# The output product of a fused attention and feed-forward kernel by Strassen's seven products

## The chip, the cores and the metric

One Trainium2 chip, one core of it. The metric is device time in microseconds (us) of one execution, the median of several runs. Engines are named as the profile names them: PE (matmuls), PEld (its weight loads), DVE (vector), ACT (scalar), POOL (GpSimd), and SP, whose queue issues the loads and stores.

## The reference

A decayed linear attention (retention) over 4 batches, 8 heads, 768 tokens, 64 channels a head, and then a bilinear feed-forward over all 3072 tokens:

```python
for t in range(S):
    state = gamma[None, :, None, None] * state + np.einsum('bhd,bhe->bhde', k[:, :, t], v[:, :, t])
    y[:, :, t] = scale * np.einsum('bhd,bhde->bhe', q[:, :, t], state)
...
a = x @ w_a          # x: 3072 x 512, w_a and w_b: 512 x 1536
b = x @ w_b
return (a * b @ w_out).astype(np.float32)     # w_out: 1536 x 512
```

Inputs and output are float32; the kernel multiplies in bfloat16 and accumulates in float32.

## The kernel before, in words

The 3072 tokens are 24 slots of 128. `TILES = [4, 2, 2, 2, 2, 4, 4, 4]` groups them into eight tiles, numbered J = 0 to 7, of 512 or 256 tokens. Everything is written out once in Python; `seq` ties each instruction to the one before it on its engine, so that every engine runs its instructions in the order of the program, and what sets that order is where a call stands.

A tile has two parts. **Its blocks**: for each of the 12 slices `ft` of the 1536 hidden channels, `ffn_a` makes four matmuls into a PSUM bank and ACT copies the result to `asb` (L540); `ffn_g` makes four more and DVE multiplies them with `asb` into `ht` (L551). **Its out part**: `ffn_out` (L566) makes, for each slot, 12 matmuls of 512 columns (`ht` against `wo_bf`), and ACT copies the bank to `osb` (L180), which SP stores. The tags of PSUM allow three banks for all of `a`, `g`, `o` and half of the state products (pool `psff`, `bufs=3`): a new product can start only when the reader of the bank that it takes is done.

The attention of two slots is a `turn` (L354), put between such calls by the table `ahead`. On PE it takes the old pair's products with the states (`inter`, twice) and within the chunk (`intra`), and the new pair's state products (`chunk_states`) and scores. On DVE it leaves a tiny copy that orders two groups of matmuls (`fenced`, L297), three or four running sums of states (`sums`, L269) and two masks (`aT`, L285). The casts of the sums to `gst` (mostly ACT) and the two copies of the attention's output to `xt` (`leave`, L343) go to a list, `later`, that `catch_up` empties at the next `ffn_out`, or two at a time at each `ft`. `xt[J]` is what the blocks of tile J read. Slots 10 and 11, for instance, are attended in a turn in the out part of tile 3 and are tile 4.

Loads of the weights go through staging tiles of the pool `wstage` (`wst`), which POOL casts to bfloat16; those of `w_out` by `cast_o`, before the blocks of tile 1. The order is: attention of the first slots and the blocks of tile 0; the blocks of tile 1; the out parts of tiles 0 and 1; and then for each tile 2 to 7 its blocks and its out part.

Of the kernel before, what the change touches and what calls it, by code (L numbers as in the profile page):

```python
# [16 lines left out]
PAIRS = 3  # L17
# [6 lines left out]
def kernel(  # L24
# [57 lines left out]
    def load_slot(t, names="kqv"):  # L82
        b, ci = divmod(t, NCH)
        for nm in names:
            if t % 2 == 0:
                whole[nm] = raw.tile([P, 2, H, D], F32, tag=nm + "f", name=nm + "f")
            raws[nm, t] = whole[nm][:, t % 2]
            s = {"k": k, "q": q, "v": v}[nm][b, :, ci * P : (ci + 1) * P, :]
            seq(nc.sync.dma_start(out=raws[nm, t], in_=s.rearrange("h p d -> p h d")))
# [46 lines left out]
    def tables(pattern, channel):  # L136
        posp = const.tile([P, NCH, 1], F32, name=f"posp{channel}")
        seq(nc.gpsimd.iota(posp, pattern=pattern, base=-MID, channel_multiplier=channel,
                           allow_small_or_imprecise_dtypes=True))
        earg = const.tile([P, NCH, H], F32, name=f"earg{channel}")  # L140
        seq(nc.vector.tensor_tensor(earg, posp.to_broadcast([P, NCH, H]),
                                    lgr.to_broadcast([P, NCH, H]), op=ALU.mult))
        ktab = const.tile([P, NCH, H, 1], F32, name=f"ktab{channel}")
        qtab = const.tile([P, NCH, H, 1], F32, name=f"qtab{channel}")
        seq(nc.scalar.activation(ktab[:, :, :, 0], earg, AF.Exp, scale=-1.0))
        seq(nc.scalar.activation(qtab[:, :, :, 0], earg, AF.Exp, bias=bq))
        tabs.append((ktab, qtab))

    tables([[2 * P, PAIRS], [1, 2], [0, 1]], 2)
# [15 lines left out]
    def late_tables():  # L165
        seq(nc.gpsimd.memset(mask, 1.0))
        for c in range(2):
            mc = mask[64 * c : 64 * c + 64]
            seq(nc.gpsimd.affine_select(out=mc, in_=mc, compare_op=ALU.is_ge, fill=0.0, base=0,
                                        pattern=[[0, 1], [1, D]], channel_multiplier=-1))  # L170
        tables([[P, NCH], [0, 1]], 1)
# [4 lines left out]
    wo_bf = wpool.tile([P, NFT, DM], BF16, name="wo_bf")  # L176
# [13 lines left out]
    def cast_o(j):  # L190
        cast(nc.gpsimd, wo_bf[:, j * FPO : (j + 1) * FPO, :], wst["o", j])
# [41 lines left out]
    def half(i):  # L233
        return slice(64 * i, 64 * i + 64)

# [37 lines left out]
    def scores(n):  # L273
        at = psat.tile([P, 2, 2, HP, D], F32, tag="at", name="at")
        for s in range(2):
            for hp in range(HP):
                for c in range(2):
                    for r in range(2):
                        seq(nc.tensor.matmul(at[half(c), r, s, hp, :],  # L279
                                             kqT[n + s][half(r), 0, hp, half(c)],  # L280
                                             kqT[n + s][half(r), 1, hp, half(c)],
# [28 lines left out]
    def inter(o, swap, y):  # L310

        for s in range(2):
            for j in range(2):
                for r in range(2):
# [4 lines left out]
                    for hp in (2 * j, 2 * j + 1):  # L319
                        into(o, c, r, seq(nc.tensor.matmul(  # L320
                            y[c][half(hp % 2), s, 2 * r + j, :], gst[(2 * t + c) % 8][half(r), hp, :],
                            kqT[t][half(r), 1, hp, half(c)], stop=y is not ys[o],
# [13 lines left out]

    def leave(o, c, apart):
        J, i = where[o]
        if i == 0 and c == 0:
            xt[J] = xtp.tile([P, KT, 4 * P], BF16, tag="xt", name="xt")  # L340
        dst = xt[J][:, :, i * P : (i + 2) * P].rearrange("p k (s c n) -> p c s k n", s=2, c=2)[:, c]
        if apart is None:
            seq(nc.scalar.copy(dst, ys[o][c]))  # L343
        else:
            on, off = slice(2 - 2 * c, 4 - 2 * c), slice(2 * c, 2 * c + 2)
            part = tra.tile([P, 2, 2, D], F32, tag="kq"[c] + "T2", name="part", bufs=2)
            seq(nc.scalar.copy(part, apart[c][:, :, on]))
            for s in range(2):
                seq(nc.vector.tensor_tensor(dst[:, s, on], ys[o][c][:, s, on], part[:, s], op=ALU.add))
                seq(nc.scalar.copy(dst[:, s, off], ys[o][c][:, s, off]))  # L350
# [128 lines left out]
    def leave2(u, on):  # L479
        J, i = where[2 * u]  # L480
        if i == 0 and J not in xt:
            xt[J] = xtp.tile([P, 4, KT, P], BF16, tag="xt", name="xt")
        for c, eng in enumerate(on):
            if eng is None:
                continue
            cast(eng, xt[J][:, i + c].rearrange("p k (m par) -> p k par m", par=2),
                 ys[u][c].rearrange("p k (par m) -> p k par m", par=2))

    def leave_apart(u, apart):

        J, i = where[2 * u]
        dst = xt[J][:, i + 1].rearrange("p k (m par) -> p k par m", par=2)
# [5 lines left out]
        seq(nc.vector.tensor_copy(dst[:, 2:], y[:, 2:]))  # L498

    def xcols(J, kt, c0, c1):  # L500
        if J < 2:
            return xt[J][:, c0 // P : c1 // P, kt, :]
        return xt[J][:, kt, c0:c1]
# [61 lines left out]

    def ffn_out(J, i):  # L566
        store()
        catch_up()
        n0 = (sum(TILES[:J]) + i) * P
        osb = wstage.tile([P, DM], F32, tag="w" + "ab"[i % 2], name="osb")  # L570
        ends = J == len(TILES) - 1 and i == TILES[J] - 1
        cols = [(0, DM // 2), (DM // 2, 3 * DM // 4), (3 * DM // 4, DM)] if ends else [(0, DM)]
        for c0, c1 in cols:
            o = psff.tile([P, DM], F32, tag="ff", name="o")[:, : c1 - c0]
            for ft in range(NFT):
                seq(nc.tensor.matmul(o, ht[J][:, ft, i * P : (i + 1) * P], wo_bf[:, ft, c0:c1],  # L576
                                     start=(ft == 0), stop=(ft == NFT - 1)))
            cast(nc.vector if c0 == DM // 2 else nc.scalar, osb[:, c0:c1], o)
            if c0 == DM // 2:
                continue  # L580
            b0 = DM // 2 if c0 else 0
            dst, src = out[n0 : n0 + P, b0:c1], osb[:, b0:c1]
            if J < len(TILES) - 2:
                held.append((dst, src))
            else:
                seq((nc.scalar if ends and not c0 else nc.sync).dma_start(out=dst, in_=src))
# [116 lines left out]
    def run(*at):  # L703
        for fn, *what in ahead.pop(at, []):
            fn(*what)
        if len(at) == 2:
            ffn_ab(*at)
        else:
            ffn_out(at[0], at[2])

    for ft in range(NFT):
        run(1, ft)
    for J in range(len(TILES)):
        if J > 1:
            for ft in range(NFT):
# [38 lines left out]
```

## Time and profile before

| | |
|---|---|
| Time of three runs | 223.96, 224.16, 224.42 us; median 224.16 |
| Span of the profiled execution | 222.2 us, granted clock 1.000 |
| Profiled execution's own time | not listed apart; the median lies 1.96 us above the span |
| PE busy | 214.4 us (96%) |
| DVE, ACT, POOL busy | 96.8, 93.7, 79.5 us |
| Chain that ended last | PE 92%; `g` 28%, `a` 28%, `o` 28% |

Busy time is the time in which an engine ran at least one instruction. A row of a group gives the count, the busy time in us and the mean duration of one in ns; for a matmul that duration holds the passage through the array, so neighbours overlap, and the rate is read from the distance of starts. After "|" stands the idle time of the engine ahead of the group and what ended it.

### The profile page before, as it was taken

To read this page: it belongs to the slowest core of one execution; us is meant where nothing else is said; L and a number is where in the kernel's file an instruction comes from. 1 tells how busy PE (TensorE), PEld (TensorE's weight loads), DVE (VectorE), ACT (ScalarE), POOL (GpSimd) and SP (SyncE) were. 2 spreads that over 40 slices of the span, in tenths; PEclk is the share of its full clock that TensorE was granted. 3 is DMA by queue.
4 is the path that set the end of the run, shared out by engine and by line. 5 is a ranking of instruction groups with operands and counts; after the bars stand their busy time and mean duration, and the time that the engine had idled before them with its cause. 6 is when DMAs were issued, how large, how long until landed. Compare 5 with 4: busy or idle time off the path is not lost.

```text
span 222.2 us, 6261 instructions
## 1 busy us (share of the span) xinstructions
PE 214.4 (96%) x2613; PEld 131.3 (59%) x2633; DVE 96.8 (44%) x199; ACT 93.7 (42%) x201; POOL 79.5 (36%) x105
## 2 busy tenths in 40 slices
PE   7799999999999999999999999999999999999994
PEld 6578655785457867867865444554444544444443
DVE  2783437641525535472475344533333621334300
ACT  3775244441535435443456333455333444333221
POOL 5557799682544335351613535350000000000000
PEclk9999999999999999999999999999999999999999
DMA  6999999999999988999969898984100012100022
GB/s 180 347 378 382 366 312 398 299 210 200 228 236 266 242 197 129 227 211 204 219 145 228 115 248 220 216 181 131 47 0 0 3 50 94 47 3 0 3 94 94
DMA packets 96124, 39.72 MB, mean 179 GB/s; under 512 B 76000, under 2 KB 91616, under 8 KB 96096
## 3 DMA queue, kind: packets, MB, share of 16 engines
q1 hardware_dynamic: 95952, 39.20, 68.5%
q8 instruction: 20, 0.33, 0.6%
q10 hardware_dynamic: 144, 0.13, 0.2%
q14 instruction: 8, 0.07, 0.1%
HBM read 28.31 MB, written 6.29 MB: 156 GB/s over the span
## 4 chain that ended last, share of the span: by engine, by line
PE 92%; DMA 3%; POOL 1%; issue 1%; DVE 1%; SPq 0%; ACT 0%; ACTq 0%; POOLq 0%
PE g L548 28%; PE a L536 28%; PE o L576 28%; DMA kf<-in_k_dram 3%; PE y L320 1%; POOL kqb L210 1%; PE at L279 1%; PE y L332 1%; PE st L255 1%; PE tp L395 1%; PE st L436 1%; DVE aT L420 1%; SPq L95 0%; PE at L408 0%; PE y L459 0%
## 5 line engine op out<-in xcount | busy, mean ns | idle before, releaser
L551 DVE TENSOR_TENSOR ht<-g,asb 128x256 bf16<-128x256 f32 (+1 forms) x98 | 53.9, 550 | 82.6 <-PE g L548 73.4
L548 PE MATMUL g<-xt,wb_bf 128*128 128x256 bf16 (+1 forms) x401 | 77.5, 317 | 0.2
L536 PE MATMUL a<-xt,wa_bf 128*128 128x256 bf16 (+1 forms) x401 | 77.2, 317 | 0.1
L540 ACT CAST asb<-a 128x256 bf16<-128x256 f32 (+1 forms) x98 | 46.3, 472 | 71.3 <-PE a L536 69.3
L576 PE MATMUL o<-wo_bf,ht 128*128 128x512 bf16 (+2 forms) x299 | 62.5, 362 | 1.4 <-issue 1.1
L536 PEld LDWEIGHTS <-wa_bf 128*128 128x128 bf16 x404 | 39.2, 98 | 23.5 <-DVE xt L182 0.4
L548 PEld LDWEIGHTS <-wb_bf 128*128 128x128 bf16 x404 | 39.4, 98 | 22.5
L576 PEld LDWEIGHTS <-ht 128*128 128x128 bf16 x312 | 28.8, 98 | 30.6
L210 POOL TENSOR_TENSOR kqb<-kf,ktab 128x512 bf16<-128x512 f32 x21 | 22.3, 1065 | 39.9 <-DMA kf<-in_k_dram 31.5
L180 ACT COPY osb<-o 128x512 f32<-128x512 f32 (+2 forms) x25 | 14.1, 564 | 36.1 <-PE o L576 27.8
L182 POOL CAST vb<-vf 128x512 bf16<-128x512 f32 x24 | 14.4, 610 | 23.0 <-DMA vf<-in_v_dram 18.5
L210 POOL TENSOR_TENSOR kqb<-qf,qtab 128x512 bf16<-128x512 f32 x21 | 22.3, 1063 | 0.1
L269 DVE TENSOR_TENSOR sums<-st,sums 128x256 f32<-128x256 f32 x30 | 12.7, 424 | 1.6
L180 ACT CAST gst<-sums 128x256 bf16<-128x256 f32 x26 | 10.4, 406 | 5.1 <-DVE sums L269 2.4
L285 DVE TENSOR_TENSOR aT<-at,mask 128x512 bf16<-128x512 f32 x18 | 11.5, 681 | 0.0
L343 ACT CAST xt<-y 128x512 bf16<-128x512 f32 x16 | 8.5, 584 | 0.7 <-PE y L332 0.7
L182 POOL CAST wo_bf<-wsto 128x1024 bf16<-128x1024 f32 x6 | 6.2, 1040 | 2.5 <-DMA wsto<-in_moe_w_out_dram 2.5
L182 POOL CAST wa_bf<-wsta 128x1024 bf16<-128x1024 f32 (+1 forms) x7 | 6.4, 919 | 1.7 <-DMA wsta<-in_moe_w_a_dram 1.6
L182 POOL CAST wb_bf<-wstb 128x1024 bf16<-128x1024 f32 (+1 forms) x7 | 6.4, 918 | 1.5 <-DMA wstb<-in_moe_w_b_dram 1.3
L395 PE MATMUL tp<-ident,kqb 128*128 128x128 bf16 x48 | 4.5, 220 | 1.6 <-DVE kqb L210 0.9
L320 PEld LDWEIGHTS <-gst 64*64 64x64 bf16 x264 | 3.7, 106 | 3.4 <-issue 3.4
L297 DVE COPY lgr<-bq 128x1 f32<-128x1 f32 x4 | 0.6, 154 | 11.2 <-PE y L320 11.2
(63 smaller groups left out, 99.2 us busy)
## 6 DMA issues: line engine op xcount, KB each, us to landing
out_dram<-osb SPq DMA_DIRECT2D x23, 256.0 KB, 2.7
kf<-in_k_dram SPq DMA_DIRECT2D x18, 256.0 KB, 4.2
qf<-in_q_dram SPq DMA_DIRECT2D x18, 256.0 KB, 4.4
vf<-in_v_dram SPq DMA_DIRECT2D x18, 256.0 KB, 4.9
wsta<-in_moe_w_a_dram SPq DMA_DIRECT2D x6, 512.0 KB, 7.6
wstb<-in_moe_w_b_dram SPq DMA_DIRECT2D x6, 512.0 KB, 7.8
wsto<-in_moe_w_out_dram SPq DMA_DIRECT2D x6, 512.0 KB, 8.5
kf<-in_k_dram SPq DMA_DIRECT2D x3, 512.0 KB, 5.9
```

The source lines that it names most:

```text
L180: seq(nc.scalar.copy(dst, src))
L182: seq(engine.tensor_copy(dst, src))
L210: seq(eng.tensor_tensor(dst, src, tab, op=ALU.mult))
L269: seq(nc.vector.tensor_tensor(new, u[c][:, s], old, op=ALU.add))
L285: seq(nc.vector.tensor_tensor(aT[n][:, r].rearrange("p s h d -> p (s h) d"), at[:, r].rearrange("p s h d -> p (s h) d"), mask.to_broadcast ...
L343: seq(nc.scalar.copy(dst, ys[o][c]))
L395: seq(nc.tensor.transpose(tp[:, m, hp, :], kqb[2 * u + par][:, i, hp, :, :], ident))
L536: seq(nc.tensor.matmul(a[:, b0 - c0 : b1 - c0], wa_bf[:, kt, fs], xcols(J, kt, b0, b1), start=(kt == 0 and b0 == c0), stop=(kt == KT - 1 a ...
L540: seq(nc.scalar.copy(asb, a))
L548: seq(nc.tensor.matmul(g[:, b0 - c0 : b1 - c0], wb_bf[:, kt, fs], xcols(J, kt, b0, b1), start=(kt == 0 and b0 == c0), stop=(kt == KT - 1 a ...
L551: seq(nc.vector.tensor_tensor(ht[J][:, ft, c0:c1], g, asbs.pop((J, ft, c0)), op=ALU.mult))
L576: seq(nc.tensor.matmul(o, ht[J][:, ft, i * P : (i + 1) * P], wo_bf[:, ft, c0:c1], start=(ft == 0), stop=(ft == NFT - 1)))
```

## The change

Tiles 1 to 7 no longer take 12 matmuls of 512 columns a slot. Two slots (256 tokens, a pair `u`) are split into even and odd tokens, the hidden channels into two halves of six slices, the output columns into two halves of 256; Strassen's method makes the 2 x 2 block product with seven half-size products instead of eight. Each product is six matmuls of 256 columns. They are called P1 to P7 here, in the order in which `ffn_fast` has them:

- P1 (bank R1) and P2 (bank R6) take `ht` as it is. ACT copies P1 to `snap` (snapshot 0), and DVE adds P2 and it into `osb`.
- P3 goes on top of P1 in R1, with the second sum of `ht` halves; ACT takes snapshot 1. P4 (bank R5), with the first sum; snapshot 2.
- P5 on top in R1, with the third sum; DVE adds it and snapshot 2. P6 on top in R5, with the fourth; DVE adds it and snapshot 1. P7 on top in R1, with `ht` as it is; ACT copies it to `osb`.

So a product that goes on top waits for the reader of what was there: P3 for snapshot 0, P5 for snapshot 1, P6 for snapshot 2, P7 for DVE's add of P5.

The four sums of `ht` halves (`hsum`, bfloat16) are DVE's: the first two in pieces among the last blocks of the tile (`sums12`), the others per pair ahead of it (`sums34`). The four combinations of the halves of `w_out` (`wt_bf`) are made once, by `combine_o`: four DVE instructions and an ACT cast for each of six slices, two slices among the blocks of tile 1, four behind the first two out products of tile 0 (which keeps the old `ffn_out`). `later` is emptied one entry at a time between products (`catch_up(1)`), and wholly at the end of a pair. A turn that stood ahead of an odd slot of a pair now stands inside it, between P3 and P4 (tiles 1, 2 and 4). So that even and odd tokens lie apart, `q` of the late slots is loaded by two DMAs instead of one (even and odd tokens), `queries` reads the turned `q` in two runs of 32, and the copies to `xt` are written in that order; a store is one of 512 KB a pair instead of two of 256 KB.

```diff
@@ load_slot
+            if nm == "q":
+                s = s.rearrange("h (n par) d -> par n h d", par=2)
+                for par in range(2):
+                    seq(nc.sync.dma_start(out=raws[nm, t][64 * par : 64 * par + 64], in_=s[par]))
...
+    def combine_o(j):
+        st = wst["o", j].rearrange("p r (c d) -> p r c d", c=2)
+        b11, b12, b21, b22 = st[:, 0, 0], st[:, 0, 1], st[:, 1, 0], st[:, 1, 1]
+        tmp = tra.tile([P, 2, DH], F32, tag="aT", name="tmp")
+        seq(nc.vector.tensor_tensor(tmp[:, 0], b12, b11, op=ALU.subtract))
+        seq(nc.vector.tensor_tensor(tmp[:, 1], b22, tmp[:, 0], op=ALU.subtract))
+        seq(nc.vector.tensor_tensor(wt_bf[:, j, 2], b22, b12, op=ALU.subtract))
+        seq(nc.vector.tensor_tensor(wt_bf[:, j, 3], b21, tmp[:, 1], op=ALU.subtract))
+        seq(nc.scalar.copy(wt_bf[:, j, :2], tmp))
...
+    def sums12(J, f0, f1):
+        if f0 == 0:
+            hsum[J] = [new_hsum(i) for i in range(2)]
+        s = [x[:, f0:f1, : TILES[J] // 2] for x in hsum[J]]
+        seq(nc.vector.tensor_tensor(s[0], rows(J, 0, 1, f0, f1), rows(J, 1, 1, f0, f1), op=ALU.add))
+        seq(nc.vector.tensor_tensor(s[1], s[0], rows(J, 0, 0, f0, f1), op=ALU.subtract))
+
+    def sums34(J, u):
...
+        seq(nc.vector.tensor_tensor(s[2], at[0], at[1], op=ALU.subtract))
+        seq(nc.vector.tensor_tensor(s[3], at[2], s[1], op=ALU.subtract))
...
+    def ffn_fast(J, u, between=None):
+        store()
+        catch_up(1)
...
+        R1 = bank()
+        product(R1, J, u, ("h", 0, 0), (0, 0), True)
+        seq(nc.scalar.copy(snap[:, 0], R1[:, :DH]))
+        catch_up(1)
+        R6 = bank()
+        product(R6, J, u, ("h", 1, 0), (0, 2), True)
+        seq(nc.vector.tensor_tensor(osb[:, 0, :DH], R6[:, :DH], snap[:, 0], op=ALU.add))
+        catch_up(1)
+        product(R1, J, u, ("s", 1), (1, 1), False)
+        seq(nc.scalar.copy(snap[:, 1], R1[:, :DH]))
+        if between:
+            between()
+        else:
+            catch_up(1)
+        R5 = bank()
+        product(R5, J, u, ("s", 0), (1, 0), True)
+        seq(nc.scalar.copy(snap[:, 2], R5[:, :DH]))
+        catch_up(1)
+        product(R1, J, u, ("s", 2), (1, 2), False)
+        seq(nc.vector.tensor_tensor(osb[:, 1, DH:], R1[:, :DH], snap[:, 2], op=ALU.add))
...
+        catch_up(1)
+        product(R5, J, u, ("s", 3), (0, 3), False)
+        seq(nc.vector.tensor_tensor(osb[:, 0, DH:], R5[:, :DH], snap[:, 1], op=ALU.add))
...
+        catch_up(1)
+        product(R1, J, u, ("h", 1, 1), (1, 3), False)
+        seq(nc.scalar.copy(osb[:, 1, :DH], R1[:, :DH]))
+        catch_up()
...
+            if J == 1 and ft in (5, 9):
+                combine_o(ft // 4 - 1)
+            if J and TILES[J] == 2 and ft in (8, 10, 11):
+                sums12(J, *{8: (0, 3), 10: (3, 5), 11: (5, 6)}[ft])
+            if J and TILES[J] == 4 and ft in (7, 9, 10, 11):
+                sums12(J, *{7: (0, 2), 9: (2, 4), 10: (4, 5), 11: (5, 6)}[ft])
...
+        for u in range(TILES[J] // 2):
+            sums34(J, u)
+            visit(J, "o", 2 * u)
+            key = (J, "o", 2 * u + 1)
+            ffn_fast(J, u, (lambda: visit(*key)) if key in ahead else None)
```

How the order moves is shown at three places; a row is one instruction, or several alike, in its engine's order, with output, input and shape.

ACT at the blocks of tile 1 and the start of the out part of tile 0, before:

```order
L180 CAST xt<-y 128x4x2x64
L540 CAST asb<-a 128x256 x12
L180 COPY osb<-o 128x512 x2
L180 CAST gst_161<-sums 128x256
L180 CAST gst_162<-sums 128x256
```

And with the change (`tmp` and `wt_bf` are those of `combine_o`):

```order
L195 CAST xt<-y 128x8x64
L575 CAST asb<-a 128x256 x6
L217 CAST wt_bf<-tmp 128x512
L575 CAST asb<-a 128x256 x4
L217 CAST wt_bf<-tmp 128x512
L575 CAST asb<-a 128x256 x2
L621 COPY osb<-o 128x512
L217 CAST wt_bf<-tmp 128x512 x2
```

The copies `asb` of `ft` 6 and 10 now stand behind a cast that reads what DVE makes.

ACT from the blocks of tile 2 to the first out product of tile 3, before (`xt` is the pair of copies that the next tile's blocks read, `lgr` the ordering copy of a turn):

```order
L540 CAST asb<-a 128x256 x12
L180 COPY osb<-o 128x512
L180 CAST gst_161<-sums 128x256
L180 CAST gst_162<-sums 128x256
L343 CAST xt<-y 128x2x4x64 x2
L180 COPY osb<-o 128x512
L540 CAST asb<-a 128x256 x12
L297 COPY lgr<-bq 128x1
L180 CAST gst_157<-sums 128x256
L180 CAST gst_158<-sums 128x256
L343 CAST xt<-y 128x2x4x64 x2
L180 COPY osb<-o 128x512 x2
```

And with the change:

```order
L575 CAST asb<-a 128x256 x12
L672 COPY snap<-o 128x256
L679 COPY snap<-o 128x256
L686 COPY snap<-o 128x256
L195 CAST gst_161<-sums 128x256
L195 CAST gst_162<-sums 128x256
L699 COPY osb<-o 128x256
L376 CAST xt<-y 128x2x8x32 x2
L575 CAST asb<-a 128x256 x12
L326 COPY lgr<-bq 128x1
L195 CAST gst_157<-sums 128x256
L672 COPY snap<-o 128x256
```

In tile 2 the two copies to `xt` moved from ahead of the last output copy to behind it; in tile 3 a `gst` cast stands ahead of snapshot 0.

DVE from the end of the blocks of tile 4 through its out part, which holds two turns, before:

```order
L551 TENSOR_TENSOR ht<-g,asb 128x256 x12
L269 TENSOR_TENSOR sums<-st,sums 128x256 x4
L285 TENSOR_TENSOR aT<-at,mask 128x512 x2
L182 CAST gst_163<-sums 128x256
L182 CAST gst_156<-sums 128x256
L297 COPY lgr<-bq 128x1
L269 TENSOR_TENSOR sums<-st,sums 128x256 x3
L285 TENSOR_TENSOR aT<-at,mask 128x512 x2
```

And with the change, from the last `ht` on (`hsum` are the sums of `ht` halves, `osb<-o,snap` the adds of `ffn_fast`):

```order
L586 TENSOR_TENSOR ht<-g,asb 128x256
L638 TENSOR_TENSOR hsum<-ht 128x128
L639 TENSOR_TENSOR hsum<-hsum,ht 128x128
L646 TENSOR_TENSOR hsum<-ht 128x6x128
L647 TENSOR_TENSOR hsum<-ht,hsum 128x6x128
L298 TENSOR_TENSOR sums<-st,sums 128x256 x4
L314 TENSOR_TENSOR aT<-at,mask 128x512 x2
L676 TENSOR_TENSOR osb<-o,snap 128x256
L197 CAST gst_163<-sums 128x256
L197 CAST gst_156<-sums 128x256
L326 COPY lgr<-bq 128x1
L298 TENSOR_TENSOR sums<-st,sums 128x256 x3
```

Four sums of `ht` stand between the last `ht` and the turn's state sums, and the add of P2 ahead of the two `gst` casts.

187 lines of the change are left out of this document (120 added, 67 removed).

## The prediction

> **What bounds the kernel now.** The page first: shares of busy time, the slices, the chain.
>
> ```profile
> PE 214.4 (96%) x2613; PEld 131.3 (59%) x2633; DVE 96.8 (44%) x199; ACT 93.7 (42%) x201; POOL 79.5 (36%) x105
> PE   7799999999999999999999999999999999999994
> PEclk9999999999999999999999999999999999999999
> PE 92%; DMA 3%; POOL 1%; issue 1%; DVE 1%; SPq 0%; ACT 0%; ACTq 0%; POOLq 0%
> ```
>
> PE is full from the third slice to the last at full clock, and is 92% of the chain: every matmul less shortens the kernel by its length, and every wait of PE lengthens it. DVE and ACT stand under half, but that is a mean over the span; what counts is the few us of each out part.
>
> The groups with shapes kept apart then give the prices.
>
> ```profile
> L576 PE MATMUL o<-wo_bf,ht 128*128 128x512 bf16 x263 | 59.9, 379 | 1.4 <-issue 1.1
> L551 DVE TENSOR_TENSOR ht<-g,asb 128x512 bf16<-128x512 f32 x46 | 31.8, 692 | 55.1 <-PE g L548 55.1
> L551 DVE TENSOR_TENSOR ht<-g,asb 128x256 bf16<-128x256 f32 x52 | 22.1, 425 | 27.5 <-PE g L548 18.3 <-ACT asb L540 9.2
> L540 ACT CAST asb<-a 128x256 bf16<-128x256 f32 x52 | 19.4, 372 | 23.5 <-PE a L536 22.6 <-DVE ht L551 0.6
> L180 ACT COPY osb<-o 128x512 f32<-128x512 f32 x23 | 13.5, 586 | 34.4 <-PE o L576 26.1 <-DMA out_dram<-osb 4.0 <-DMA kf<-in_k_dram 2.0
> L269 DVE TENSOR_TENSOR sums<-st,sums 128x256 f32<-128x256 f32 x30 | 12.7, 424 | 1.6
> L180 ACT CAST gst<-sums 128x256 bf16<-128x256 f32 x26 | 10.4, 406 | 5.1 <-DVE sums L269 2.4 <-DVE sums L267 1.5
> L180 ACT CAST vb<-vf 128x512 bf16<-128x512 f32 x1 | 0.6, 622 | 0.0
> L180 ACT COPY osb<-o 128x256 f32<-128x256 f32 x1 | 0.4, 373 | 0.7 <-PE o L576 0.7
> ```
>
> Before, an out product waits for nothing: 1.4 us idle over all of them.
>
> **What is saved.** The rate of 512-column matmuls is read from the distance of two output copies, that of 256-column ones from the chain; the last rows of this fence are stretches of a 256-column tile.
>
> ```profile
> 211.32 0.58 ACT L180 COPY osb<-o 128x512 f32<-128x512 f32 x1 [2.87 <-PE o L576]
> 213.91 0.59 ACT L180 COPY osb<-o 128x512 f32<-128x512 f32 x1 [2.00 <-DMA out_dram<-osb]
> 68.92 0.44 PE g L548 x4
> 73.29 0.44 PE g L548 x4
> 41.00 0.60 PE L536 MATMUL a<-xt,wa_bf 128*128 128x256 bf16 x4
> 41.43 0.60 PE L548 MATMUL g<-xt,wb_bf 128*128 128x256 bf16 x4
> 41.63 0.37 ACT L540 CAST asb<-a 128x256 bf16<-128x256 f32 x1 [0.54 <-PE a L536]
> 41.87 0.60 PE L536 MATMUL a<-xt,wa_bf 128*128 128x256 bf16 x4
> 42.14 0.42 DVE L551 TENSOR_TENSOR ht<-g,asb 128x256 bf16<-128x256 f32 x1 [0.49 <-PE g L548]
> 39.27 0.74 DVE L182 CAST xt<-y 128x512 bf16<-128x512 f32 x1
> 40.07 0.61 PE L536 MATMUL a<-xt,wa_bf 128*128 128x256 bf16 x4
> ```
>
> A slot's 12 matmuls take 2.59 us, a pair's 24 take 5.18. From 68.92 to 73.29 lie five rounds of a and g, 40 matmuls: 0.109 us each, weight loads included. Seven products of six are 42 x 0.109 = 4.59, one product 0.655. Saved: 0.59 a pair, **5.9 us** over ten pairs.
>
> **What a reader costs.** ACT starts 0.20 after the matmuls' last issue (41.43 to 41.63), DVE 0.27 (41.87 to 42.14), and PE goes on 0.06 after a DVE end (39.27 + 0.74 = 40.01, 40.07). So a snapshot returns a bank after 0.20 + 0.37 + 0.06 = 0.63 us, just within the 0.655 of the product between; DVE's add after 0.27 + 0.42 + 0.06 = 0.75. P7 therefore waits 0.1 even on idle engines: 0.5 us in the five or six pairs where nothing worse holds it.
>
> **The sums of halves.** No row before multiplies or adds two bf16 tiles of SBUF. From the two `ht` rows, 256 elements more cost 267 ns: 1.04 ns each beside a fixed 158, so 768 elements cost 0.96 at one a step. Against it stand rows of copies:
>
> ```profile
> L182 DVE COPY qT<-tp 128x512 bf16<-128x512 bf16 x2 | 0.8, 424 | 0.8 <-PE tp L395 0.8
> L182 DVE CAST gst<-sums 128x256 bf16<-128x256 f32 x7 | 1.8, 290 | 0.0
> ```
>
> 512 bf16 elements in 424 ns (not 692), 256 in 290 (not 425): two a step. I take two: 158 + 768 x 0.52 = 0.56 us, 0.36 for 384, 0.29 for 256, 0.23 for 128; the ends of the range are 0.96, and 0.29 for any of them.
>
> The Trainium skill (VectorE: DVE Perf Modes, the perf-mode tier table) gives `tensor_tensor` twice the rate when all tensors are bf16 in SBUF, and the plain rate for any PSUM operand. By that rule the sum is the forecast; by the `ht` row it is the first rival. No run here shows it yet.
>
> **Where PE waits.** The bank rule and the order decide it; times from rows of turns:
>
> ```profile
> 81.48 0.32 PE L320 MATMUL y<-kqT,gst 64*64 64x64 bf16 x16
> 81.86 0.15 DVE L297 COPY lgr<-bq 128x1 f32<-128x1 f32 x1 [2.36 <-PE y L320]
> 82.11 1.34 DVE L269 TENSOR_TENSOR sums<-st,sums 128x256 f32<-128x256 f32 x3
> 82.14 0.33 PE L320 MATMUL y<-kqT,gst 64*64 64x64 bf16 x16
> 82.95 2.54 PE L576 MATMUL o<-wo_bf,ht 128*128 128x512 bf16 x11 [0.16 <-issue]
> 83.34 1.06 ACT L343 CAST xt<-y 128x512 bf16<-128x512 f32 x2
> 83.37 1.28 DVE L285 TENSOR_TENSOR aT<-at,mask 128x512 bf16<-128x512 f32 x2
> 113.64 1.87 DVE L269 TENSOR_TENSOR sums<-st,sums 128x256 f32<-128x256 f32 x4
> 182.95 0.29 DVE L349 TENSOR_TENSOR xt<-y,part 128x128 bf16<-128x128 f32 x1 [4.16 <-ACT part L347]
> 185.42 0.27 ACT L350 CAST xt<-y 128x128 bf16<-128x128 f32 x1 [0.36 <-DVE xt L349]
> ```
>
> A turn takes PE 1.45 us (81.48 to 82.95), DVE 1.34 or 1.87 and 1.28.
>
> 1. *Weights combined among the blocks of tile 1.* `asb` of the next slice stands on ACT behind the `wt_bf` cast, and that behind DVE's second subtraction. After the last `g` (zero): `ht` until 0.69, two subtractions (0.42 each, the price of `sums`) until 1.56, the cast about 0.6 (the price of `vb`) until 2.2, `asb` 2.57, PE 2.63. The product that needs that bank would start after three groups of 0.436, at 1.31: 1.3 lost, and 1.5 at the second place, where sums of 384 stand ahead: **2.9**. The four combinations in the out part of tile 0 cost nothing: their 4 x 1.6 us of DVE and the turn behind them end before P1 of tile 1 at 11.
> 2. *`xt` behind the last output copy*, tiles 2 and 4. The next blocks wait for 0.20 + 0.37 + 2 x 0.53 (two copies in 1.06) + 0.06 = 1.7 after P7: **3.4**. Before, an out product of 2.59 covered it.
> 3. *`gst` ahead of snapshot 0*, tiles 3 to 6. Tile 3, from the last `g`: `ht` 0.69, sums of 128 1.15, of 768 2.25, first state sum 2.65, `gst` 3.05, snapshot 3.45, PE 3.5. PE comes to P3 after 1.45 + 1.31 = 2.76: 0.7 lost, in tile 4 too; in tiles 5 and 6 `ht` takes 0.69 and the sums are of 256, 1.1 each: **3.6**.
> 4. *Turn inside the pair*, P7. After its start in tile 1, DVE: 0.63 + 1.87 + 1.28 + 0.42 + 0.06 = 4.26; PE 1.45 + 3 x 0.655 = 3.42: 0.85. Tile 2 about 0.5 (its ordering copy stands behind the sums), tile 3 0.4 and tile 4 0.2 from the backlog of item 3: **1.95**.
> 5. *Second turn of tile 4*. It opens with a `gst` that DVE casts at 2.25 + 1.87 + 1.28 + 0.42 + 0.29 = 6.1; PE is there at 2.76 + 0.7 + 0.655 = 4.1: **2.0**.
> 6. *Second turns of tiles 5 and 6*. Tile 5: the ordering copy comes behind two sums, at 8.45 where PE wants it at 7.86: 0.6. Tile 6: the last `xt` pieces (182.95 to 185.69, half of them ahead of each snapshot) hold snapshots 0 and 1: about 1.1. **1.7**.
> 7. *Sums of 384* behind `ft` 8 hold the bank of `g` 0.13 in tiles 2 to 4: **0.4**.
>
> With P7's 0.5: 16.45 lost, 5.9 saved, **10.5 us longer**. At nothing I cost: the tail (the same 128 KB go last, a copy of 256 for one of 128: 0.1), the even and odd runs in `queries` (as many columns), the extra loads of `q` (the same bytes; prefetched a stage ahead), and `xt` in plain runs instead of the 0.74 of the row at 39.27 (0.1 or 0.2 back).
>
> The median of 224.16 lies 1.96 above the profiled span of 222.2; added to the median, **234.7 us**. A measurement of this kernel tells about 0.2% (0.45 us) from no change.
>
> **The rivals.** *DVE makes one element a step.* Each sum of 768 costs 0.4 more, of 384 0.2. Out parts of tiles 2 to 4 pay 0.94 each, tiles 5 and 6 1.07 and 0.8, tile 7 0.7, the sums behind `ft` 8 0.4 in four tiles: 2.8 + 3.7 + 0.7 + 1.6 = 8.8, 243.5. For it the `ht` rows, against it the copies. 0.17.
>
> *POOL and DVE hold each other up.* Where both read two tiles of SBUF, one slows:
>
> ```profile
> L210 POOL TENSOR_TENSOR kqb<-kf,ktab 128x512 bf16<-128x512 f32 x21 | 22.3, 1065 | 39.9 <-DMA kf<-in_k_dram 31.5 <-PE a L536 4.6 <-PE y L332 3.1
> ...
> 7.81 0.69 DVE L210 TENSOR_TENSOR kqb<-kf,ktab 128x512 bf16<-128x512 f32 x1 [0.16 <-DMA kf<-in_k_dram]
> 7.93 1.47 POOL L210 TENSOR_TENSOR kqb<-kf,ktab 128x512 bf16<-128x512 f32 x1 [3.67 <-DMA kf<-in_k_dram]
> ```
>
> POOL takes 1.47 there against a mean of 1.065 over the group; DVE keeps its 0.69. If DVE paid those 40% on the sums and combinations up to tile 5, half of the 8.8: 239. 0.08.
>
> *Faster: the waits fall away, the columns stay saved.* Place: items 1 to 3, 9.9 us of order on ACT. The change is faster once all waits together are under 5.9, 0.59 a pair. If sums and casts end before PE comes (DVE's sums at 0.29, and ACT reaching its casts during the turns), only P7's 0.1 and a remainder of 2 to 3 are left: 5.9 - 3.5, 221.8. Against it: item 2 alone takes 3.4 and needs no unknown price. 0.12. Landing within 0.2%: 0.03.
>
> **How the numbers follow.** The forecast holds 0.60. Sums at 0.29 take some 3.5 from items 3 to 6 (231), waits a third shorter 5.5 (229): its own range is 229 to 240. The range of 8 in 10 takes in the first rival: 227 to 245. Faster 0.12, same 0.03, slower 0.85.
>
> **What would show it.** A 256-column out product at 0.109 a matmul and PE busy some 6 us less, with 16 us more of idle PE, put down to ACT `snap`, `asb` and `xt` and DVE `osb`; `hsum` of 768 at 0.56; two gaps of 1.3 to 1.5 in the blocks of tile 1, two of 1.7 ahead of tiles 3 and 5. PE idle in the out parts under 6 us in all would make the prediction wrong, and so would an `hsum` of 768 at 0.96.

## The result and the profile after

The changed kernel takes 244.85 us (median of four, 241.96 to 247.67) against 224.06 before (four, 223.93 to 224.42): ratio 1.0875, interval 1.0814 to 1.0937. Forecast were 234.7 in a range of 227 to 245: the sign held, the size was 10 us short. The profiled execution (247.67 us, span 246.0) is the slowest of its four and counts as a slow run, which the ratios in this document leave out and the medians do not; so what follows is read mostly from a second one of the same kernel, the control below (span 242.0 of 243.76 us).

First the page of the changed kernel: busy times, the granted clock in 40 slices, the chain.

```profile
PE 219.1 (89%) x2786; PEld 149.5 (61%) x2789; DVE 151.7 (62%) x321; ACT 97.5 (40%) x226; POOL 82.7 (34%) x107
PEclk9999999997999999999997799999999999999998
PE 53%; DVE 11%; DMA 4%; ACT 3%; issue 2%; SPq 2%; DVEq 0%
```

PE fell from 92% of the chain to 53%, DVE's busy time rose by 55 us, and there are slices in which the clock was not full, of which the kernel before had none. The control's groups by shape (busy, mean ns) and its list of waits (in total, times, longest) name the places:

```profile
L586 DVE TENSOR_TENSOR ht<-g,asb 128x512 bf16<-128x512 f32 x46 | 31.8, 691 | 43.7 <-PE g L583 43.1
L298 DVE TENSOR_TENSOR sums<-st,sums 128x256 f32<-128x256 f32 x30 | 12.7, 423 | 1.4
L647 DVE TENSOR_TENSOR hsum<-ht,hsum 128x768 bf16<-128x768 bf16 x10 | 6.3, 635 | 0.0
L646 DVE TENSOR_TENSOR hsum<-ht 128x768 bf16<-128x768 bf16 x10 | 5.9, 588 | 0.0
```

```profile
PE g L583 <- ACT asb L575: 3.7, 2, 1.9
PE o L657 <- ACT snap L672: 3.2, 5, 0.9
PE a L571 <- ACT xt L376: 2.9, 2, 1.4
PE y L349 <- ACT xt L376: 1.4, 1, 1.4
PE o L657 <- DVE osb L689: 0.8, 2, 0.6
PE a L571 <- DVE ht L586: 0.7, 3, 0.3
PE o L657 <- DVE sums L298: 0.7, 1, 0.7
```

The waits stand where the prediction put them (`asb`, snapshot 0, `xt`). `ht` and `sums`, which have one operand in PSUM, cost what they did before (691 and 423 ns); the sums of halves do not keep to one price.

What the waits do not show comes out by stage, from the starts of PE's rows in the timelines (us; an out part begins with the turn that stands ahead of it; the last column adds up the prediction's own terms stage by stage):

| Stage | Before | After | Control | Control less before | Predicted |
|---|---|---|---|---|---|
| to the blocks of tile 0 | 16.05 | 17.66 | 17.55 | +1.50 | 0 |
| blocks of tile 0 | 23.06 | 24.45 | 24.54 | +1.48 | 0 |
| blocks of tile 1 | 11.49 | 15.53 | 16.23 | +4.74 | +2.9 |
| out parts of tiles 0 and 1 | 17.72 | 20.29 | 20.71 | +2.99 | +0.4 |
| blocks of tiles 2 to 4 | 31.64 | 32.06 | 32.69 | +1.05 | +0.4 |
| out part of tile 2 | 6.52 | 7.86 | 7.86 | +1.34 | +1.7 |
| out part of tile 3 | 6.52 | 9.22 | 7.28 | +0.76 | +0.6 |
| out part of tile 4 | 7.80 | 14.97 | 12.55 | +4.75 | +4.1 |
| out part of tile 5 | 13.05 | 15.29 | 13.66 | +0.61 | +0.6 |
| out part of tile 6 | 12.34 | 13.25 | 13.25 | +0.91 | +1.0 |
| out part of tile 7, to the end | 13.67 | 13.07 | 13.34 | -0.33 | -1.1 |

The blocks of tiles 5 to 7 are equal to 0.1. Tiles 2 to 6 came out near the forecast in the control; of the 9.2 us that the forecast lacked, 7.4 lie ahead of tile 2 and 0.8 in tile 7. The first execution does not agree so well: its out parts of tiles 3 to 5 cost 12.1 us more than before, where 5.3 were forecast.

### The profile page after: what moved, and what is told of

The parts are those of the page before. It is cut to its first block, busy times and chain, and to the rows that moved or that the text cites. A ratio compares the mean times of both kernels' runs of the same rounds, so it can differ in the third digit from the quotient of the medians.

```text
span 246.0 us, 6767 instructions
## 1 busy us (share of the span) xinstructions
PE 219.1 (89%) x2786; PEld 149.5 (61%) x2789; DVE 151.7 (62%) x321; ACT 97.5 (40%) x226; POOL 82.7 (34%) x107
## 4 chain that ended last, share of the span: by engine, by line
PE 53%; DVE 11%; DMA 4%; ACT 3%; issue 2%; SPq 2%; DVEq 0%
PE a L571 19%; PE g L583 19%; PE o L657 14%; DMA vf<-in_v_dram 2%; DVE hsum L647 2%; DMA kqT<-kqb 2%; DVE ht L586 2%; ACT xt L376 1%; DVE hsum L646 1%; DVE sums L298 1%; SPq L92 1%; DVE hsum L639 1%; DVE hsum L638 1%; DVE aT L314 1%; PE y L361 1%
## 5 line engine op out<-in xcount | busy, mean ns | idle before, releaser
L657 PEld LDWEIGHTS <-hsum 128*128 128x128 bf16 x240 | 23.7, 101 | 11.3 <-issue 7.4
L657 PE MATMUL o<-wt_bf,hsum 128*128 128x256 bf16 x180 | 23.7, 285 | 6.4 <-ACT snap L672 6.0
L236 POOL TENSOR_TENSOR kqb<-qf,qtab 128x512 bf16<-128x512 f32 x21 | 23.4, 1118 | 9.2 <-DMA qf<-in_q_dram 8.9
L197 POOL CAST vb<-vf 128x512 bf16<-128x512 f32 x24 | 15.1, 639 | 29.0 <-DMA vf<-in_v_dram 20.9
L657 PEld LDWEIGHTS <-ht 128*128 128x128 bf16 x180 | 17.0, 97 | 5.4 <-issue 2.1
L657 PE MATMUL o<-wo_bf,ht 128*128 128x256 bf16 x120 | 14.8, 273 | 0.0
L618 PE MATMUL o<-wo_bf,ht 128*128 128x512 bf16 x46 | 11.9, 412 | 0.1
L639 DVE TENSOR_TENSOR hsum<-hsum,ht 128x256 bf16<-128x256 bf16 (+3 forms) x24 | 9.4, 393 | 0.9
L657 PE MATMUL o<-wt_bf,ht 128*128 128x256 bf16 x60 | 8.2, 271 | 1.8 <-DVE osb L689 1.7
L638 DVE TENSOR_TENSOR hsum<-ht 128x256 bf16<-128x256 bf16 (+3 forms) x24 | 9.1, 377 | 0.9
L618 PEld LDWEIGHTS <-ht 128*128 128x128 bf16 x48 | 5.0, 106 | 6.3 <-issue 1.7
```

Of the source, the lines that this page charges most:

```text
L197: seq(engine.tensor_copy(dst, src))
L236: seq(eng.tensor_tensor(dst, src, tab, op=ALU.mult))
L638: seq(nc.vector.tensor_tensor(s[0], rows(J, 0, 1, f0, f1), rows(J, 1, 1, f0, f1), op=ALU.add))
L639: seq(nc.vector.tensor_tensor(s[1], s[0], rows(J, 0, 0, f0, f1), op=ALU.subtract))
L657: seq(nc.tensor.matmul(R[:, :DH], lhs, (wo_bf, wt_bf)[w][:, f, m, :], start=(first and f == 0), stop=(f == NH - 1), skip_group_check=True))
```

## The experiments

Theories: **order** (the prediction's: PE waits where an order on ACT and DVE makes it); **lock** (a DVE instruction that reads SBUF alone stands still until the POOL instruction that was running ends, and POOL likewise); **clock** (PE's waits lower its clock); and, from the first two rows of the table, **alignment** (where the tiles lie in SBUF).

### control: the changed kernel again

> The changed kernel once more, for a second trace. Before its run the stage table (starts of the blocks and out parts on PE) has it 3.0 us behind already at the blocks of tile 1 (42.11 against 39.11). If the change's loads cause that, it is there again; if it was that one execution's DMA, the blocks of tile 1 start at 39.1 to 39.6 and the span is that much shorter. Clock theory (PE's granted clock falls for some us after a stretch in which PE waited much): spans between 240 and 246 go with granted clocks between 1.000 and 0.976, about 2.4 us per 0.01.

243.75 us (242.80 to 245.32), ratio 1.0881 (1.0834 to 1.0928). The 3.0 us at the start are there again, so they belong to the change. Its clock, in windows of 2 us (PE, PEld, DVE, ACT, POOL busy; then the granted clock, the DMA share and GB/s):

```profile
54.00:56.00 2.00, 1.51 (x13) 1.06 (x11) 1.87 (x5) 0.01 (x1) 1.60 (x3) 1.00 0.97 131
56.00:58.00 2.00, 0.38 (x3) 0.30 (x3) 1.71 (x4) 1.16 (x3) 0.36 (x1) 0.94 0.64 115
58.00:60.00 2.00, 2.00 (x7) 0.78 (x6) 1.83 (x8) 0.00 (x0) 0.00 (x0) 0.50 0.90 200
60.00:62.00 2.00, 1.84 (x7) 0.83 (x7) 1.97 (x5) 0.00 (x0) 1.06 (x1) 0.71 1.10 179
```

PE waits 1.92 us for `asb` up to 57.62, and then runs at 0.50 until about 61. From 132 to 136 the clock is at 0.71 and 0.50 again, this time behind waits of 0.32 and 1.44, while a wait of 1.82 that ended at 51.64 left it at 1.00. A mean clock of 0.986 over 242 us is 3.4 us of lost PE time. By these windows an estimated 1.4 us of it lie in the out parts of tiles 0 and 1 (58.32 to 60 at 0.50, 60 to 62 at 0.71), which lacked 2.6, and 1.7 in the out part of tile 4; without them the row of tile 4 would stand at about 3 us, so that its agreement with the 4.1 of the forecast is in part luck. The expected slope did not hold: spans of 240.3, 243.1, 243.1 and 246.0 went with 1.000, 0.997, 0.993 and 0.976, and the control's 243.5 and 242.0 both with 0.986.

### halves: POOL's late multiplications in two pieces

```diff
...
-            scaled(nc.gpsimd, t, 0)
-            scaled(nc.gpsimd, t, 1)
+            for i in range(2):
+                for r in range(2):
+                    scaled(nc.gpsimd, t, i, r)
```

> Each of POOL's late multiplications of 128x512 is written as two of 128x256; nothing else changes. Lock theory (a DVE instruction that reads its operands from SBUF stands still until the POOL instruction that was running ends, and POOL likewise): the longest sum of 768, 1.40 us where the undisturbed ones take 0.55, can only stretch by half as much, to 0.9 to 1.0, and the time falls by 1 to 2 us against the control. The rival that DVE is slowed by a share (40%) while POOL runs: the stretched sums stay near 0.8 to 1.4, as many of them, and the time stays, or rises by POOL's added overhead.

Sums of 768 by instruction (ns: least, median, longest), the control and then halves:

```profile
L646 DVE TENSOR_TENSOR hsum<-ht x10: 546/550/932, 72.8 to 233.1; 128x768 bf16<-128x768 bf16 x10
L647 DVE TENSOR_TENSOR hsum<-ht,hsum x10: 546/551/1396, 73.2 to 233.6; 128x768 bf16<-128x768 bf16 x10
```

```profile
L649 DVE TENSOR_TENSOR hsum<-ht x10: 546/551/981, 71.3 to 232.5; 128x768 bf16<-128x768 bf16 x10
L650 DVE TENSOR_TENSOR hsum<-ht,hsum x10: 550/551/967, 71.8 to 233.0; 128x768 bf16<-128x768 bf16 x10
```

The undisturbed sum takes 0.55; the longest fell from 1.40 to 0.98, as the lock has it and a slowing by a share has not. The timeline of the changed kernel's first execution shows one such meeting:

```profile
108.12 0.55 DVE L646 TENSOR_TENSOR hsum<-ht 128x768 bf16<-128x768 bf16 x1
108.31 1.26 POOL L236 TENSOR_TENSOR kqb<-qf,qtab 128x512 bf16<-128x512 f32 x1 [1.47 <-DMA qf<-in_q_dram]
108.59 1.40 DVE L647 TENSOR_TENSOR hsum<-ht,hsum 128x768 bf16<-128x768 bf16 x1
```

POOL starts while the first sum runs and takes 1.26 instead of 1.04; the second sum starts while POOL runs, and ends at 109.99, 0.42 after POOL's end at 109.57. Each waits for the other's instruction. It is so throughout: of the control's 68 sums of halves, of all sizes, ten are stretched, and each of the ten starts while a POOL instruction runs; none of the other 58 does. The time, 243.34 (ratio 1.0855, 1.0832 to 1.0877), cannot be told from the control's, so the expected gain of 1 to 2 us failed to come; that other waits covered the sums' delay is argued here, not shown.

### nosum: the sums left out

```diff
-                lhs = hsum[J][left[1]][:, f, u]
+                r, par = left[1] % 2, left[1] // 2
+                lhs = ht[J][:, NH * r + f, (2 * u + par) * P : (2 * u + par + 1) * P]
...
-            sums34(J, u)
```

(The calls of `sums12` are left out in the same way.)

> The sums of ht halves are left out (products 3 to 6 read ht itself, as many columns; the output is another). By the prediction's items 3 and 7 and the backlog in 4 and 5, sums of 0.56 cost about 5 us: 237. With the lock (sums of 768 at up to 1.4 us and DVE casts held up behind them) 8 to 9 us: 233.5. Rival that order alone holds PE and the sums lie beside it: within 2 us of the control.

239.72, ratio 1.0687 (1.0656 to 1.0718): 4.0 us less than the control, nearest to the prediction's 5, under the lock's 8 to 9 and over the 2 of a rival in which the sums cost nothing. PE's waits for snapshot 0 fall from 3.2 to 0.2; those for `asb` and `xt` stay, and one appears that the control does not have:

```profile
PE g L583 <- ACT asb L575: 3.0, 2, 1.7
PE at L308 <- DMA kqT<-kqb: 2.9, 2, 1.8
PE a L571 <- ACT xt L376: 2.9, 2, 1.4
```

Once PE comes earlier, it finds the transposes of `kqb` late. That points back to the DMAs.

### order123: items 1 to 3 by order alone

```diff
...
-            if J == 1 and ft in (5, 9):
-                combine_o(ft // 4 - 1)
+            if J == 1 and ft < 8:
+                combine_o(ft // 4, [ft % 4])      # one DVE instruction a slice
+            if J == 1 and ft in (3, 7):
+                combine_o(ft // 4, [4])           # the cast on ACT
...
-        store()
-        catch_up(1)
+        store()
...
-(2, "o", 1): [(turn, 10, 8, D_), (casts, 13)]
+(2, "o", 1): [(turn, 10, 8, D_, True), (casts, 13)]
```

(`catch_up(1)` behind snapshot 0 goes too, and the turn in tile 4 is given `True`, which puts the copies to `xt` at the head of the list.)

> Items 1 to 3 taken away by order alone: the combinations of two slices of w_out stand one DVE instruction at a time among the blocks of tile 1, with a cast that waits for nothing; the xt copies of the turns in tiles 2 and 4 stand ahead of the gst casts in the list; no gst cast stands ahead of snapshot 0 or right behind it. By the prediction these three are worth 2.9 + 3.4 + 3.6 = 9.9 us: 232. By the lock theory item 3 comes back as DVE's own backlog (snapshot 0 is not what ends last, P5 to P7 wait for DVE): 6 to 7 us, 235 to 236. The blocks of tile 1 (15.5 us after, 11.5 before) should fall to 11.5 to 12 in both, and the waits of 1.44 ahead of tiles 3 and 5 should go.

244.22, ratio 1.0910 (1.0840 to 1.0981): nothing gained, against both expectations. Yet two of the three came near what was forecast: the blocks of tile 1 take 12.89 (16.23), the out part of tile 2 6.25 (7.86). The out parts of tiles 3, 4 and 5 gave it back, with 8.58, 13.30 and 17.05. Tile 5 in PE's timeline:

```profile
161.28 1.48 PE L663 MATMUL o<-wt_bf,hsum 128*128 128x256 bf16 x12 [1.76 <-DVE sums L304]
...
165.60 0.28 PE L355 MATMUL y<-kqT,gst 64*64 64x64 bf16 x11 [1.44 <-ACT xt L382]
...
173.12 1.02 PE L577 MATMUL a<-xt,wa_bf 128*128 128x512 bf16 x4 [1.44 <-ACT xt L382]
```

The `gst` casts taken from around snapshot 0 stand ahead of snapshot 1 and behind snapshot 2 now, and the copies to `xt` of a turn ahead of a pair, which come last in the list, slid behind the pair's last output copy: two new waits of 1.44. P4, the row at 161.28, waits for DVE's state sums, whose bank it takes. Here, removing a place where the list is emptied only moved the wait to whatever is last in the list.

### aligned and before_shift: 32 bytes

In both the same line is added among the constants:

```diff
     zero = const.tile([P, 4 * P], BF16, name="zero")
+    const.tile([P, 8], F32, name="pad")
```

The change also makes two more small tables for `q` (24 and 192 bytes a partition, the first rounded up to 32), which the list of the change does not name. Every tile that is made behind them starts 224 bytes further on; the 12288 bytes of `wt_bf` add a multiple of 256 for most.

> An unused tile of 32 bytes a partition is added among the constants, so that every later tile of SBUF starts at the address modulo 64 that it has in the kernel before (the change's two small tables for q shift them by 224 bytes); nothing else. In the traces of the changed kernel the first loads, of the same bytes, run at 291 GB/s where before they run at 347, and the blocks of tile 1 start 3.0 us later in all five of its traces. Alignment theory: 347 GB/s again, the blocks of tile 1 at 39.1 to 39.5, 3 us or a little more off the time: 240 to 241. Rival (the two DMAs for q, or the extra tables, hold the queue): no change, 243 to 244.

> The kernel before with the same unused tile of 32 bytes: its tiles of SBUF start 32 bytes off a multiple of 64. Alignment theory: its first loads fall to 291 GB/s and it takes 3 us longer, 227. Rival: 224.1 as before.

The rate of the loads in 40 slices of the first 32 us, one row each of before, control, aligned and before_shift:

```profile
GB/s 0 0 57 172 347 347 347 346 348 347 346 348 346 348 363 384 367 384 384 384 388 383 402 361 370 389 383 388 384 381 396 352 346 348 348 237 322 308 223 360
```

```profile
GB/s 0 0 57 164 333 326 294 287 292 290 291 290 291 287 291 292 309 330 348 348 348 348 348 348 362 333 341 353 348 347 351 347 349 355 335 330 301 298 291 261
```

```profile
GB/s 0 0 47 161 340 345 348 347 348 344 348 348 345 348 378 360 371 388 383 385 385 385 393 362 380 385 385 384 383 388 388 355 349 348 348 275 264 328 202 340
```

```profile
GB/s 0 0 50 163 327 310 309 291 295 288 291 291 289 290 292 290 307 332 344 351 347 349 348 347 364 333 344 350 348 347 349 347 349 353 339 331 301 298 289 283
```

The rate follows the 32 bytes in both kernels: 347 GB/s where, by the sizes of the tiles ahead of them, the staging tiles start at multiples of 256 bytes, 290 where they are shifted by 32 (before_shift) or 224 (the change). before_shift takes 234.58, ratio 1.0458 (1.0403 to 1.0513): 10 us, not 3. Its trace is the fastest of its four executions (231.67 us, clock 1.000 against 0.991 in the others) and shows 7.8 us of it: the blocks of tile 1 start 3.1 us late, the out parts of tiles 0 and 1 take 1.8 and that of tile 4 2.2 more, with waits for `kqT` and POOL's `vb`. aligned has its start back (blocks of tile 1 at 38.93), but not its time: 244.87, ratio 1.0874 (1.0785 to 1.0962). The out parts of tiles 0 and 1 now take 22.10 and those of tiles 2 and 4 8.89 and 15.28: PE comes earlier, to the same waits on ACT and DVE, some of them longer (2.27 us for `sums` where the control has 0.65). Its clock was lower too, 0.972 to 0.979 in its four executions against 0.986 to 0.993 in the control; 0.012 of 243 us is an estimate of up to 2.9 us, about what the start had gained.

### filled: matmuls in the waits

```diff
+    def fill(n, bank):
+        for _ in range(n):
+            seq(nc.tensor.matmul(bank, zero[:, :P], zero[:, :DH], start=True, stop=True, skip_group_check=True))
...
+        if J == 1 and ft in (7, 11):
+            fill(12, whole_a[:, DH:])
...
+        if J == 4:
+            fill(14, R6[:, DH:])
         product(R1, J, u, ("s", 1), (1, 1), False)
...
+            if J == 4:
+                fill(8, R6[:, DH:])
             between()
```

> The changed kernel with matmuls that compute nothing put where PE waits: 12 each in the blocks of tile 1 ahead of the two waits for asb, 14 ahead of P3 and 8 ahead of the turn in tile 4 (0.109 us each, 5 us in all, into halves of banks that nothing uses). Clock theory (waits of PE make the granted clock fall to half for 3 to 4 us, at 57 and at 132 us): the clock is 1.000 or close to it in every run, the spread of the runs falls from 2.5 us to under 1, and the time falls by 1 to 2 us, 242, although work was added. Rival (the clock falls for another reason): clock 0.98 to 0.99 as in the control, and the added work costs 1 to 4 us: 245 to 247.

The clock came as its theory has it: 1.000, 1.000 and 0.998 in three of four runs (0.980 in one). The time did not: 247.33, ratio 1.0988 (1.0931 to 1.1045), by the ratios 2.4 us more than the control, as the rival had it. The windows in which the control stood at 0.71 and 0.50, in the control and then in filled:

```profile
132.00:134.00 2.00, 1.73 (x121) 1.60 (x121) 1.67 (x7) 0.22 (x1) 0.00 (x0) 0.71 0.90 155
134.00:136.00 2.00, 2.00 (x14) 1.45 (x11) 1.58 (x3) 0.51 (x2) 0.00 (x0) 0.50 0.99 278
```

```profile
132.00:134.00 2.00, 0.57 (x6) 0.51 (x6) 1.78 (x5) 0.00 (x0) 0.49 (x1) 1.00 0.88 119
134.00:136.00 2.00, 2.00 (x21) 1.79 (x19) 0.00 (x0) 0.19 (x1) 0.68 (x1) 1.00 0.86 191
```

The filler (L593) stood in front of P3 and waited for a bank itself, and P3 of tile 3, which has no filler, waited as long:

```profile
PE o L665 <- ACT snap L680: 5.0, 4, 2.4
PE o L593 <- DVE osb L684: 2.6, 1, 2.6
```

At both waits, of 2.4 and 2.6 us, filled's clock stayed at 1.00; so did aligned's at waits of 1.92 and 2.06. In halves and spread_nopad it fell to 0.5 from 8 to 11 us, where no wait ahead was longer than 0.9. That PE's waits lower the clock is therefore not shown, and what the lower clock costs is not settled by this run either.

### spread, spread_nopad and spread_halves: the order mended

spread is aligned with the combinations of order123, all places of `catch_up` kept, and

```diff
-                eng = nc.vector if s and n in (8, 10, 12, 14) else nc.scalar
+                eng = nc.scalar
...
-(3, "o", 0): [(turn, 12, 10), (casts, 16)]
+(3, "o", 0): [(turn, 12, 10, A_, True), (casts, 16)]
...
-            sums34(J, u)
             visit(J, "o", 2 * u)
...
+            if J and TILES[J] == 2 and ft in (6, 7):
+                sum3(J, 3 * (ft - 6), 3 * (ft - 5))
+            if J and TILES[J] == 2 and ft == 9:
+                sum4(J, 0, 3, slice(0, 1))
```

(in every turn `True`; the rest of the fourth sum behind the add of P2).

> A version meant to win: the 32 bytes; the combinations of two slices one DVE instruction at a time among the blocks of tile 1; every turn's copies to xt ahead of its gst casts in the list, and all gst casts on ACT; the third sum among the blocks at ft 6 to 8, half or a third of the fourth at ft 8 or 9, the rest of the fourth behind the add of P2. By order alone (prediction): the two waits of 1.44 ahead of tiles 3 and 5 and those for snapshot 0 go, and 5 us of columns stay saved against about 3 of waits: 222 to 224. With the lock (sums, combinations and POOL's late work in each other's way): 3 to 4 us more, 226 to 228. Both expect the blocks of tile 1 at 12 to 13 us and the out parts of tiles 2 to 6 each at or under the time before plus 1.

> The version spread without the 32 bytes. Alignment theory, by what the same shift did to the kernel before (10 us): 240 to 242, 3.0 us of it up to the blocks of tile 1 and the rest as waits for kqT and POOL's vb in the out parts of tiles 0 and 4. Rival (only the first loads are slower and the rest was this kernel's order): 235 to 236.

> The version spread with POOL's late multiplications in halves of 128x256. In spread the blocks of tiles 1, 2 and 3 take 3.3, 1.5 and 1.3 us longer than before, with PE waiting for ht that stands behind sums and combinations on DVE. Lock theory: these waits come from DVE standing still behind POOL for up to 1.05 us and fall to about half with POOL's instructions: 230 to 231. Rival (DVE simply has too much to do there): 232 to 233.

spread takes 232.37, ratio 1.0326 (1.0270 to 1.0382), some 12 us under aligned, with a clock of 0.999 or 1.000 in three of its four runs. The out parts of tiles 2 to 6 are at 6.59, 5.99, 9.03, 12.34 and 12.23; the waits for `xt` are gone, and those for snapshot 0 but for 0.2. What is left, worst first:

```profile
PE a L578 <- DVE ht L593: 4.3, 5, 1.5
```

and why, in its timeline (blocks of tile 1):

```profile
50.52 1.04 POOL L243 TENSOR_TENSOR kqb<-kf,ktab 128x512 bf16<-128x512 f32 x1 [1.30 <-DMA kf<-in_k_dram]
50.80 0.98 DVE L643 TENSOR_TENSOR hsum<-ht 128x384 bf16<-128x384 bf16 x1
51.52 1.16 POOL L243 TENSOR_TENSOR kqb<-qf,qtab 128x512 bf16<-128x512 f32 x1
51.81 1.08 DVE L644 TENSOR_TENSOR hsum<-hsum,ht 128x384 bf16<-128x384 bf16 x1
...
52.82 0.41 DVE L593 TENSOR_TENSOR ht<-g,asb 128x256 bf16<-128x256 f32 x1
...
53.28 0.60 PE L578 MATMUL a<-xt,wa_bf 128*128 128x256 bf16 x4 [1.49 <-DVE ht L593]
```

Two sums of 384, 0.36 each when alone, take 0.98 and 1.08 beside POOL, and `ht`, for which PE waits, stands behind them. With POOL's work in halves the same wait falls to

```profile
PE a L581 <- DVE ht L596: 1.4, 5, 0.4
```

and spread_halves takes 229.23, ratio 1.0208 (1.0166 to 1.0250): by the ratios 2.6 us less than spread, a little more than the lock's 1.4 to 2.4. What did not show in the time of halves shows here. spread_nopad takes 237.63, ratio 1.0587 (1.0553 to 1.0621): by the ratios 5.9 us for the 32 bytes in this order, between the two expectations. Its trace has 3.1 us of waits for `kqT` and 1.2 for POOL's `vb`, of which spread's has none, and a clock of 0.986 against 0.999; what each is worth was not separated.

### parity_only and late3: how much of the change can win

```diff
     def outs(J):
+        if J < 8:                      # late3: J < 5
+            for i in range(TILES[J]):
+                visit(J, "o", i)
+                ffn_out(J, i)
+            return
```

> No Strassen at all: the changed kernel's layout (two DMAs for q, split runs, xt by parity, one store a pair) and the 32 bytes, with 12 matmuls of 512 columns a slot in every tile and no sums and combinations; the very last store is one of 512 KB, so the out part of tile 7 ends 1 to 2 us later than before. By the prediction the layout costs nothing: every stage up to the out part of tile 6 within 0.3 us of before, 225 to 226. Rival: the two DMAs for q delay the transposes, with waits for kqT of 1 us or more in the out parts of tiles 0 and 4.

> Strassen in tiles 5 to 7 alone, with the 32 bytes; the combinations of w_out are made of the bfloat16 weights by DVE in the first six slices of tile 5; turns and sums of these tiles as in the version spread; tiles 0 to 4 keep 12 matmuls of 512 columns a slot. In spread the out parts of tiles 5, 6 and 7 take 0.7, 0.1 and 0.4 us less than before; if nothing is lost elsewhere, 223.0, 0.5% under before. Lock theory: POOL is busy until slot 23 is done in tile 6, so one or two of the combinations stand still up to 0.85 us, which the 1.0 us of slack that DVE has in each slice of a 512-token tile hides: same number. Against it: the parity layout costs something of itself (then no gain, 224 to 225).

parity_only takes 226.56, ratio 1.0127 (1.0069 to 1.0185). 1.06 us of it lie in the tail as expected, but 0.88 and 0.44 in the out parts of tiles 0, 1 and 4, where PE's timeline has the rival's waits, smaller than expected:

```profile
65.92 0.32 PE L309 MATMUL at<-kqT 64*64 64x64 bf16 x16 [0.72 <-DMA kqT<-kqb]
...
119.15 0.32 PE L309 MATMUL at<-kqT 64*64 64x64 bf16 x16 [0.29 <-DMA kqT<-kqb]
```

late3 takes 225.97, ratio 1.0080 (1.0050 to 1.0110): not a win either. Its tile 7 saves 0.7, its out part of tile 5 loses 1.3 (0.68 for DVE's state sums, 1.05 that the trace calls issue), and the out parts of tiles 0 and 1 lose 0.4, where only the layout differs. No version here beat the kernel before; the best with Strassen in all of tiles 1 to 7 stands 2% above it.

## Why the prediction was right, and where it was short

**The sign.** The sum rested on waits that outweigh 0.5 us a pair, and they did: PE idles 23.1 us in the control (242.0 less 218.9) against 7.8 before, 15.3 more where 16 were forecast. The range held by luck: 244.85 lies 0.15 under its upper end, which was set for the first rival, and the forecast's own range of 229 to 240 was missed.

**What is saved.** Two P1 rows of tile 7, where nothing else holds, give the pair:

```profile
228.66 1.47 PE L657 MATMUL o<-wo_bf,ht 128*128 128x256 bf16 x12
...
233.34 1.47 PE L657 MATMUL o<-wo_bf,ht 128*128 128x256 bf16 x12
```

4.68 us against 5.18: 0.50 saved, not 0.59. The tail, at nothing in the prediction, takes 0.7 of what two pairs save there (-0.33 instead of -1.0). The forecast that PE would be 6 us less busy failed: 218.9, and still 214.4, as before, in spread at a clock of 0.999. So the missing 10 us appear as PE's busy time, not as more idle time than forecast. About 3.4 of the difference is the clock; the rest is not settled.

**Items by the control's waits.** Item 1: 3.7 against 2.9, same place and releaser; DVE's combinations took up to 1.32 instead of 0.42. Its second half, that the four combinations behind tile 0's products cost nothing, failed: 0.7 for `sums` (and 2.3 in aligned). Item 2: 2 x 1.44 = 2.9 against 3.4. Item 3: 3.2 against 3.6 (6.0 in the other execution). Item 4: 0.8 (0.65 in tile 1, where 0.85 was forecast) against 1.95; too high. Item 5: right in size (1.44 against 2.0), wrong in cause: the turn waits for ACT's copies to `xt`, which it empties from the list first, not for DVE's `gst`. Item 6: 0.3 in tile 5 against 0.6, and 0.6 behind snapshots in tile 6 against 1.1 (0.24 of it within item 3's 3.2). Item 7: 0.7 against 0.4. Taken together, the items were sized about right in the control.

**The sums** cost 0.55 when alone: the forecast's 0.56, and not the first rival's 0.96. So 243.5, which is nearly the measured time, is the right number from a mechanism that did not occur.

**The step that failed** is what the sum put at nothing. *The tables* are not in its list "At nothing I cost" at all: they move the tiles behind them by 224 bytes, which alone costs 3.0 us ahead of tile 1, and 5.9 us in spread; in the changed kernel itself, taking the shift away (aligned) gained no time. The trace before could not show it, though the addresses could be counted. *The layout* (the runs in `queries` and the extra loads of `q`) is in the list: about 1.3 us in the out parts of tiles 0, 1 and 4 (parity_only). Which of these, with the clock, makes up the 9.2 us was not separated. Then *the second rival*, mis-sized: DVE and POOL do not slow each other by 40%, each waits for the other's instruction, 0.4 to 0.9 us at a time; shown by halves, and worth 2.6 us between spread and spread_halves. The rows at 7.81 and 7.93 of the kernel before fit this lock already: POOL's 0.4 over its usual time lie within the 0.57 us that DVE still had to run (7.81 + 0.69 less 7.93). I read a delay as a rate. The Trainium skill (GPSIMD Engine Reference, 8. Key points) says that GpSimd shares its SBUF interfaces with VectorE, with contention against instructions with two SBUF inputs or in a two-port mode. For two SBUF inputs the traces agree (the ten stretched sums of the control), and add the price, which the page does not give; no run here singles out the two-port mode.

**Not in the prediction at all**: the clock. The Trainium skill (TensorE: Matmul & The Clock Gate, Part 1) has the array at half rate after an idle window of about 3.4 us. The 0.50 agrees; the length does not show here, since the clock fell behind a wait of 1.92 us in the control and stayed full at one of 2.57 in filled.

The costs do not add up one by one: 10 us for the shift in the kernel before, 5.9 in spread, nothing in the changed kernel. Where two waits end at the same place, taking away one moves nothing; so the sum over items was near for each stage with one cause, and none of halves, order123 and aligned gained by itself.

## What to carry to other kernels

Count what a change does to the addresses of tiles, not only to the instructions: in spread, two small tables ahead of the pools cost as much as the whole saving (5.9 us against ten pairs of 0.5), and 32 unused bytes put it back. Before giving DVE new work that reads SBUF alone, look at what POOL does at that time, and cut POOL's instructions to the wait that the path can bear. When a kernel waits in many places, mend the order as a whole before judging one item: order123 and aligned alone gained nothing, together with the moved sums they are part of 12 us.

## What the hardware showed that was not expected

- Loads into staging tiles that start 32 or 224 bytes past a multiple of 256 run at 290 GB/s instead of 347, in two kernels, and 32 bytes more or less decide it. Which multiple is needed (64, 128 or 256) was not tried.
- A DVE instruction whose operands are all in SBUF, the float32 subtractions (0.42 to 1.32) and the bfloat16 sums (0.55 to 1.40) alike, and a POOL instruction exclude each other; means of `ht` and `sums`, which have one operand in PSUM, did not move (691 and 423 ns).
- The granted clock fell to 0.50 for some 4 to 6 us in some executions of the changed kernel and not in others (means of 0.976 to 1.000). It did so behind PE waits of 1.92 us (control) and 2.20 us (after), and stayed at 1.00 at waits of 2.36 and 2.57 us (filled); what decides it is open.
